# Down products of a fused attention and feed-forward kernel read in two 64-row halves of the array, and key loads with fewer transfers

## The chip, the cores and the metric

The kernel runs on one core of a Trainium2 chip. The metric is the device time of one execution in microseconds (us). Before the change the median of three runs is 2585.47 us, from 2585.27 to 2585.91. The engines are TensorE (PE; its weight loads are shown apart as PEld), VectorE (DVE), ScalarE (ACT), GpSimd (POOL) and SyncE (SP), which here issues the transfers. PSUM has eight banks; a product of up to 512 columns in float32 fills one.

## The reference, cut to what matters

```python
x = A_x                                       # 1 x 2048 x 576
xn = layernorm(x)
q, k, v = split(xn @ wqkv)                    # 32 heads of 18
o = softmax(q @ k.T * 18 ** -0.5) @ v         # per head
s = o @ wo                                    # 576 x 576
f = (gelu(xn @ w_gate) * (xn @ w_up)) @ w_down   # 576 -> 4608 -> 576
out = x + s * silu(f)
```

The product with `w_down` is the "down product" of this document.

## The kernel before

**Precision.** Every factor of a product is held as a high part and a low part in the PE's fast float32 type, and a product is three products: high by high, low by high, high by low. For queries and keys the three stand below one another in one operand of 54 rows (MROW = 3 * 18), and two heads share a tile of 128 rows, one in rows 0 to 63, one in rows 64 to 127.

**Tiles and loops.** Tokens are taken in NB = 4 batches of TB = 512, each of four tiles of 128. F = 4608 is taken in NF = 144 pieces of 128 columns over the four batches: one `section` for each. A prologue (line 162 and others) computes queries, keys and values. Then nine sections (the list FIRST) run ahead of the attention, with the maxima of its first unit among them; then NU * NA = 128 sections (the range ATT) run with the attention spread among them; then the last seven (the epilogue).

**A section** is 27 pairs of gate and up products (line 388), where the gate product reads rows 0 to 63 and the up product rows 64 to 127, each 512 columns wide. Among them stand, in ATT, 16 pairs of one score product (line 729, its exponential on ACT at line 730) and one maximum product (line 698, reduced on DVE at line 699), also one in each half. Behind a section stand, in this order on PE: 16 value products on 32 columns of the array (line 764; a trace shows two instructions for each), at times the small product `max_end` (line 712), at times one output projection of 14 products (`project_o`, line 582), and `downs()`. PE's order is the order of the program; other engines' orders are made by a scheduler.

**The down product.** G = 2 sections make one step r of a batch (NR = 18). Behind a step, `down` is called twice, for token tiles 0 and 1 and for tiles 2 and 3. Each call computes for a tile j and a half c of the 576 outputs (288 columns) a sum of six products over 128 rows, in one PSUM bank `py`, which DVE adds to `Y` (line 432; ACT copies it at line 430 in the first step). In ATT both calls mostly come together (48 products), in other places one call comes behind one section and the other behind the next (24 products).

**Banks.** Tags: "f" has two banks (gate and up products), "m" three (maxima, `acc`, `po`, `max_end`), "s" three (scores, `py`). A tile that is asked for waits until the reader of the tile that had the bank is done.

**Transfers.** SP issues them in order. `load_k` brings a chunk of 512 keys of four heads, `load_q` the queries, one transfer for each of three parts of 18 rows (lines 662 and 687); `load_gu` (line 114) brings the weights of the next section, which POOL splits (lines 94 and 96).

The functions that the change touches:

Of the kernel before, what the change touches and what calls it, by code (L numbers as in the profile page):

```python
# [8 lines left out]
F32 = mybir.dt.float32  # L9
F32R = mybir.dt.float32r  # L10
AF = mybir.ActivationFunctionType
ALU = mybir.AluOpType
# [32 lines left out]
BANKS = {"f": 2, "m": 3, "s": 3}  # L45
# [6 lines left out]
def f(ap):  # L52
    return ap.bitcast(F32)
# [13 lines left out]
def kernel(ctx: ExitStack, tc: tile.TileContext, x, wqkv, wo, w_gate, w_up, w_down, out):  # L67
    nc = tc.nc
    x = x.rearrange("b s d -> (b s) d")
# [18 lines left out]
    identr = const.tile([P, P], F32R, name="identr")  # L88
    nc.gpsimd.tensor_copy(identr, ident)
    all_t = slice(0, TB)  # L90


    def split(hi, lo, raw, keep=lambda i: i):
# [47 lines left out]
    with tc.tile_pool(name="pro", bufs=1) as pro, tc.tile_pool(name="pps", bufs=1, space=PSUM) as pps:  # L141
# [43 lines left out]
        def norm(xr, b, between=None, behind=None):  # L185
            keep = tc.keep_in_program_order if b == 1 else lambda i: i
            st = pro.tile([P, 4, 8], F32, name="st", bufs=2)
            for j in range(4):
                bs = pro.tile([P, 2, 6], F32, name="bs", bufs=2)
                for h in range(2):  # L190
                    one = nc.vector.bn_stats(bs[:, h, :], xr[j][:, 288 * h:288 * h + 288])  # L191
                    keep(one)
                if behind and j == 0:
                    behind(one)
                nc.vector.bn_aggr(st[:, j, 0:2], bs)
            var, r, t = st[:, :, 1], st[:, :, 3], st[:, :, 4]
            nc.scalar.activation(t, var, AF.Sqrt, bias=eps)
            if between:
                between()
            nc.vector.reciprocal(r, t)  # L200
            nc.vector.scalar_tensor_tensor(t, r, -0.5, r, op0=ALU.mult, op1=ALU.mult)
            nc.vector.scalar_tensor_tensor(t, var, EPS, t, op0=ALU.add, op1=ALU.mult)
            nc.vector.scalar_tensor_tensor(r, t, 1.5, r, op0=ALU.add, op1=ALU.mult)
            for j in range(4):
                last = nc.vector.tensor_scalar(xr[j][:, 0:D], xr[j][:, 0:D], st[:, j, 0:1], st[:, j, 3:4],
                                               op0=ALU.subtract, op1=ALU.mult)
                nc.scalar.activation(xr[j][:, D:D + HR], xr[j][:, R0:D], AF.Copy)
            return last
# [42 lines left out]
        def split_qk(t, raw):  # L251
            hi, lo = (pro.tile([P, KT, P], F32R, name=f"q{m}{t}") for m in "hl")
            first = split(hi, lo, raw)
            put_qk(t, hi, lo)
            return first
# [39 lines left out]
                tc.keep_in_program_order(nc.sync.dma_start(wos[i, k * P:k * P + n, :], f(t)[0:n]))  # L295

        NQT = 2 * D // P
        def after(what, before):
            tc.add_manual_dep(what.ins, before.ins.name, mybir.DependencyInfo(
                mybir.DependencyClass.Sync, mybir.DependencyReason.DATA), reason="VectorE alone on the first x")  # L300

        raw_v, ahead_qk, QR = [], [], []
        t = ORDER[0]
        c0 = slice(t * P, (t + 1) * P)
# [17 lines left out]
        last = norm(xr, 0, first_hi, first_loads)  # L322
# [53 lines left out]
    finals = []  # L376

    def gate_up(tag):

        w, xd = FF["w"], FF["xd"]  # L380
        pg, pu = (ps.tile([P, TB], F32, name=n, tag=tag, bufs=BANKS[tag]) for n in ("pg", "pu"))
        terms = [(wp, *divmod(c, XG), xp) for c in range(NC) for wp, xp in ((0, 0), (1, 0), (0, 1))]

        def pair(i):
            wp, k, c, xp = terms[i]
            for a, o in enumerate((pg, pu)):
                rr = slice(HR * a, HR * a + HR)
                nc.tensor.matmul(o, w[1 + wp][k][rr, c, :], xd[xp][k][rr, c, :], start=(i == 0),  # L388
                                 stop=(i == len(terms) - 1))

        return [lambda i=i: pair(i) for i in range(len(terms))], pg, pu
# [6 lines left out]
    def activate(pg, pu, early):  # L398
# [13 lines left out]
            nc.vector.tensor_tensor(t1, t1, pu, op=ALU.mult)  # L412
        return t1

    def down(b, r, hs, wd, Y, js):
        for j in js:
            tt = slice(j * P, (j + 1) * P)
            for c in range(2):
                cc = slice(288 * c, 288 * c + 288)
                tag = "sf"[c if b == NB - 1 and r == NR - 1 else 0]  # L420
                py = ps.tile([P, 288], F32, name="py", tag=tag, bufs=BANKS[tag])
                n = 0
                for g in range(G):
                    hh, hl = hs[g]
                    for a, w in ((hh, wd[0]), (hh, wd[1]), (hl, wd[0])):
                        nc.tensor.matmul(py, a[:, tt], w[:, g, cc], start=(n == 0), stop=(n == 3 * G - 1))  # L426
                        n += 1
                yy = Y[:, j, cc]
                if r == 0:
                    nc.scalar.activation(yy, py, AF.Copy)  # L430
                else:
                    nc.vector.tensor_tensor(yy, py, yy, op=ALU.add)  # L432
                if b == NB - 1 and r == NR - 1:
                    finals.append((Y, j, c))
        if b < NB - 1 and r == NR - 1:
            FF["gates"] += [(b, j, c, Y) for j in js for c in range(2)]

# [70 lines left out]
    op = ctx.enter_context(tc.tile_pool(name="op", bufs=1, reuse_waits="tile"))  # L508
# [98 lines left out]
    for b in range(NB):  # L607
        last = b == NB - 1
# [8 lines left out]
        first = (b + 1) * AB + 3 if last else max((b + 1) * AB + 6, (b + 1) * NR * G - len(FIRST) + 5)  # L617
# [4 lines left out]
        for i in range(GROUPS):  # L622
            n = first + i * (1 if last else G)
# [17 lines left out]
    with tc.tile_pool(name="att", bufs=1, reuse_waits="tile") as att:  # L641
# [8 lines left out]
        def load_k(n, keep=lambda i: i, rs=(0, 1)):  # L650

            u, c = divmod(n, NA)
            if u >= NU:
                return
            cols = slice(c * TB, (c + 1) * TB)
            for r in rs:
                for a in range(2):
                    kk = f(KS[n % KB][r])[64 * a:64 * a + MROW, :]
                    h = QD * (u % NQ) + 2 * r + a
                    rows = slice(D + h * DH, D + (h + 1) * DH)  # L660
                    for n_, i in enumerate((0, 1, 0)):
                        keep(nc.sync.dma_start(kk[n_ * DH:(n_ + 1) * DH, :], qk[i, rows, cols]))

        def load_v(n):

# [11 lines left out]
        def load_q(u, rs=(0, 1)):  # L677
            j, g = divmod(u, NQ)
            cols = slice(j * TB, (j + 1) * TB)
            for r in rs:  # L680
                t = QS[u, r] = att.tile([P, TB], F32R, name=f"q{r}", bufs=3)
                for a in range(2):
                    q = f(t)[HR * a:HR * a + MROW, :]
                    h = QD * g + 2 * r + a
                    rows = slice(h * DH, (h + 1) * DH)
                    for n, i in enumerate((0, 0, 1)):
                        nc.sync.dma_start(q[n * DH:(n + 1) * DH, :], qk[i, rows, cols])
                    nc.sync.dma_start(f(t)[HR * a + MROW:HR * a + HR, :], zq)

        def max_mm(u, i, a):  # L690
# [41 lines left out]
        def lead_pair(s):  # L732

            for a in range(2):
                max_mm(*divmod(s, NS), a)
# [69 lines left out]
        slot, chunk = 0, 1  # L805
        for n, m in enumerate(FIRST):
            none = [lambda: None]
            lead = [lambda s=s: lead_pair(s) for s in range(slot, slot + m)]
            if 0 in NM:
                lead.insert(1, lambda: max_end(0))  # L810
            section((n == 2) * 5 * none + lead + (m > 0 and n != 2) * none, "s" if n == 1 else "f", lead_raw)
            if slot + m >= NS > slot:
                max_neg(0, tc.keep_in_program_order)
            slot += m
            while n > 0 and chunk < KB and chunk * SLOTS <= slot + SLOTS:
                load_k(chunk, tc.keep_in_program_order)
# [34 lines left out]
    with tc.tile_pool(name="epi", bufs=1, reuse_waits="tile") as epi:  # L851
# [4 lines left out]
        n = NU * NA  # L856
# [36 lines left out]
        for Y, j, c in finals:  # L893
            cc = slice(288 * c, 288 * c + 288)
# [7 lines left out]
        for i in range(HIND + 1, GROUPS):  # L902
            th, j, cc = late[i]
# [31 lines left out]
```

## Time and profile before

| | |
|---|---|
| median of three runs | 2585.47 us |
| the profiled execution, its own time | 2584.62 us |
| its span in the profile | 2582.7 us |
| TensorE clock granted | 1.00 |
| VectorE busy | 2010.5 us, 78% |
| ScalarE busy | 1502.5 us, 58% |
| GpSimd busy | 1389.8 us, 54% |

A row of the timeline has the start and the length in us, the engine, the line and the operation, output and inputs, and in brackets how long the engine was idle before it and what ended that. Matmuls are pipelined, so that their lengths overlap: what one costs is the distance from its start to the next start.

### The profile page before, as it was taken

How to read it: one execution, taken by the hardware profiler on the slowest of the kernel's cores; microseconds unless marked ns; L12 is line 12 of the kernel's file. 1: busy time of each engine (PE TensorE's matmuls, PEld its weight loads, DVE VectorE, ACT ScalarE, POOL GpSimd, SP SyncE). 2: the span in 40 equal slices, each digit the busy share in tenths (PEclk: the TensorE clock that was granted, in tenths of full speed). 3: DMA queues.
4: the chain of work that ended last, by engine and by line, in shares of the span. 5: the costliest groups of instructions: out<-in, count | busy, mean ns of one | idle time of the engine just before them, and what ended most of it. 6: DMA issues, size and time to landing. Idle time of an engine off the chain costs nothing.

```text
span 2582.7 us, 56466 instructions
## 1 busy us (share of the span) xinstructions
PE 2575.9 (100%) x20982; PEld 1959.8 (76%) x20982; DVE 2010.5 (78%) x3501; ACT 1502.5 (58%) x2715; POOL 1389.8 (54%) x1506
## 2 busy tenths in 40 slices
PE   9999999999999999999999999999999999999999
PEld 8888777777777777777777777777777777777778
DVE  5326888888887888888888888888888888888445
ACT  3223466666666666565667765556666765566642
POOL 2117554554566465556457565555455755555553
PEclk9999999999999999999999999999999999999999
DMA  8866443344455444544445444445445543545342
GB/s 265 267 237 162 117 104 98 102 105 105 105 135 131 110 114 105 136 111 113 127 114 133 119 125 112 125 112 133 108 109 126 141 114 104 139 110 137 78 117 59
DMA packets 394912, 326.93 MB, mean 127 GB/s; under 512 B 107980, under 2 KB 308684, under 8 KB 394640
## 3 DMA queue, kind: packets, MB, share of 16 engines
q1 hardware_dynamic: 394640, 323.32, 47.3%
q8 instruction: 168, 2.75, 0.5%
q14 instruction: 104, 0.85, 0.1%
HBM read 269.79 MB, written 52.88 MB: 125 GB/s over the span
## 4 chain that ended last, share of the span: by engine, by line
PE 99%; DVE 1%; DMA 0%; POOL 0%; ACT 0%; issue 0%; SPq 0%; DVEq 0%
PE pg L388 25%; PE py L426 18%; PE acc L764 18%; PE pu L388 10%; PE pe L729 9%; PE pm L698 9%; PE po L162 7%; PE po L582 2%; DVE mx L699 0%; PE pt L223 0%; PE pm L712 0%; DMA xx<-in_A_x_dram 0%; DVE bs L191 0%; POOL wh L94 0%; DVE m L706 0%
## 5 line engine op out<-in xcount | busy, mean ns | idle before, releaser
L730 ACT ACTIVATE pT<-pe 128x512 f32<-128x512 f32 x2048 | 1151.6, 599 | 678.4 <-PE pm L698 578.7
L699 DVE TENSOR_REDUCE mx<-pm 128x1 f32<-128x512 f32 x2048 | 1260.0, 683 | 76.4 <-PE pm L698 73.1
L388 PE MATMUL pg<-xd,wh 64*128 64x512 f32 x2592 | 935.5, 393 | 0.0
L388 PE MATMUL pu<-xd,wh 64*128 64x512 f32 x2592 | 935.1, 393 | 0.0
L698 PE MATMUL pm<-KS,q 64*128 64x512 f32 x2048 | 785.2, 388 | 0.2 <-DVE accs L770 0.2
L729 PE MATMUL pe<-q,KS 64*128 64x512 f32 x2048 | 777.9, 387 | 0.0
L94 POOL TENSOR_SCALAR wh<-raw 128x384 fp32r<-128x384 f32 x432 | 228.3, 529 | 610.2 <-PE pu L388 264.0
L388 PEld LDWEIGHTS pg<-xd,wh 64*128 64x128 f32 x2592 | 476.2, 184 | 98.5 <-issue 19.9
L388 PE MATMUL pg<-xd,wl 64*128 64x512 f32 x1296 | 502.0, 387 | 0.9 <-POOL wl L96 0.9
L388 PE MATMUL pu<-xd,wl 64*128 64x512 f32 x1296 | 501.8, 387 | 0.0
L388 PEld LDWEIGHTS pu<-xd,wh 64*128 64x128 f32 x2592 | 477.1, 184 | 22.6
L764 PE MATMUL acc<-pT,VS 128*32 128x512 f32 x4096 | 466.0, 595 | 0.0
L96 POOL TENSOR_TENSOR wl<-raw,wh 128x384 fp32r<-128x384 f32 x432 | 442.1, 1024 | 34.1
L698 PEld LDWEIGHTS pm<-KS,q 64*128 64x128 f32 x2048 | 375.7, 184 | 38.6 <-DVE mx L699 4.9
L729 PEld LDWEIGHTS pe<-q,KS 64*128 64x128 f32 x2048 | 370.1, 184 | 29.9
L432 DVE TENSOR_TENSOR Y<-py,Y 128x288 f32<-128x288 f32 x544 | 248.1, 457 | 161.1 <-PE py L426 160.8
L426 PE MATMUL py<-dh,hh 128*128 128x288 f32 x1152 | 346.0, 300 | 0.0
L426 PE MATMUL py<-dh,hl 128*128 128x288 f32 x1152 | 339.8, 295 | 0.0
L426 PE MATMUL py<-dl,hh 128*128 128x288 f32 x1152 | 339.6, 295 | 0.0
L764 PEld LDWEIGHTS acc<-pT,VS 128*32 128x32 f32 x4096 | 120.5, 109 | 274.5 <-issue 271.2
L388 PEld LDWEIGHTS pg<-xd,wl 64*128 64x128 f32 x1296 | 238.5, 184 | 31.7 <-POOL wl L96 1.2
L388 PEld LDWEIGHTS pu<-xd,wl 64*128 64x128 f32 x1296 | 238.7, 184 | 11.1
(127 smaller groups left out, 2946.5 us busy)
## 6 DMA issues: line engine op xcount, KB each, us to landing
KS<-qk SPq DMA_DIRECT2D x1536, 36.0 KB
raw<-in_B_w_gate_dram SPq DMA_DIRECT2D x144, 288.0 KB
raw<-in_B_w_up_dram SPq DMA_DIRECT2D x144, 288.0 KB
raw<-in_B_w_down_dram SPq DMA_DIRECT2D x68, 576.0 KB
VS<-vs SPq DMA_DIRECT2D x128, 152.0 KB
qk<-t SPq DMA_DIRECT2D x72, 256.0 KB
q<-qk SPq DMA_DIRECT2D x384, 36.0 KB
xd<-xhs SPq DMA_DIRECT2D x24, 384.0 KB
```

The lines of the kernel that those rows point to most:

```text
L94: first = nc.gpsimd.tensor_scalar(hi, raw, 1.0, 1.0, op0=ALU.mult, op1=ALU.mult)
L96: keep(nc.gpsimd.tensor_tensor(lo, raw, f(hi), op=ALU.subtract))
L162: nc.tensor.matmul(o, st, m, start=(i == 0), stop=(i == len(terms) - 1))
L388: nc.tensor.matmul(o, w[1 + wp][k][rr, c, :], xd[xp][k][rr, c, :], start=(i == 0), stop=(i == len(terms) - 1))
L426: nc.tensor.matmul(py, a[:, tt], w[:, g, cc], start=(n == 0), stop=(n == 3 * G - 1))
L432: nc.vector.tensor_tensor(yy, py, yy, op=ALU.add)
L582: nc.tensor.matmul(po[:, 0:288], o[x][:, k, :], ow[w][:, k, :], start=(m == 0), stop=(m == len(terms) - 1))
L698: nc.tensor.matmul(pm, QS[u, r][rr, t * P:(t + 1) * P], KS[(u * NA + c) % KB][r][rr, :], start=True, stop=True)
L699: nc.vector.tensor_reduce(MX[u][:, 2 * r + a, t, c:c + 1], pm, axis=AX.X, op=ALU.max)
L729: nc.tensor.matmul(pe, KS[(u * NA + c) % KB][r][rr, t * P:(t + 1) * P], QS[u, r][rr, :], start=True, stop=True)
L730: nc.scalar.activation(PT[u, kt][:, 2 * r + a, :], pe, AF.Exp, scale=SCALE)
L764: nc.tensor.matmul(ACC[u][32 * a:32 * a + 32, :], VS[(u * NA + c) % VB][:, v:v + 32], pt[:, a, :], start=first, stop=last, skip_group_chec ...
```

## The change

Down products up to the end of ATT (`FF["n"] <= ATT.stop`) are issued as products of 64 rows, two at a time: rows 0 to 63 into the bank of one half c, rows 64 to 127 into the bank of the other, for all six terms of a tile j; then, for both tiles of the call, the same with the halves c changed. A call holds four banks at once, whose tags are given by hand. So that both halves of the array don't write one bank at the same time, an ACT instruction (`mark`) waits for the last pair of a tile's first pass, and the first pair of its second pass waits for `mark`. The adds come behind the second pass. The sums themselves are unchanged. The last eight calls keep the old form.

For keys, the second and third part come in one transfer of 36 rows (the order of the parts changes from high, low, high to high, high, low, and for queries from high, high, low to high, low, high). In FIRST the loads of further key chunks begin one section later. `after` moves to the top of the kernel.

```diff
+    def add_down(b, r, py, Y, j, c):
+        yy = Y[:, j, 288 * c:288 * c + 288]
+        if r == 0:
+            nc.scalar.activation(yy, py, AF.Copy)
+        else:
+            nc.vector.tensor_tensor(yy, py, yy, op=ALU.add)
+        if b == NB - 1 and r == NR - 1:
+            finals.append((Y, j, c))
+
     def down(b, r, hs, wd, Y, js):
-        for j in js:
-            tt = slice(j * P, (j + 1) * P)
-            for c in range(2):
-                cc = slice(288 * c, 288 * c + 288)
-                tag = "sf"[c if b == NB - 1 and r == NR - 1 else 0]
-                py = ps.tile([P, 288], F32, name="py", tag=tag, bufs=BANKS[tag])
-                n = 0
-                for g in range(G):
-                    hh, hl = hs[g]
-                    for a, w in ((hh, wd[0]), (hh, wd[1]), (hl, wd[0])):
-                        nc.tensor.matmul(py, a[:, tt], w[:, g, cc], start=(n == 0), stop=(n == 3 * G - 1))
-                        n += 1
...
+        terms = [(a, w, g) for g in range(G) for a, w in ((0, 0), (0, 1), (1, 0))]
+
+        def product(py, j, c, i, rr=slice(0, P), start=False, stop=False):
+            a, w, g = terms[i]
+            return nc.tensor.matmul(py, hs[g][a][rr, j * P:(j + 1) * P], wd[w][rr, g, 288 * c:288 * c + 288], start=start, stop=stop)
...
+        last = len(terms) - 1
+        if FF["n"] <= ATT.stop:
+            tags = ("sssm", "sssf", "fssm")[0 if FF["n"] <= ATT.start else 1 + js[0] // 2]
+            pys = {(j, c): bank(tags[2 * (j - js[0]) + c]) for j in js for c in range(2)}
+            seen = {}
+            for swap in range(2):
+                for j in js:
+                    for i in range(len(terms)):
+                        for a in range(2):
+                            c = a ^ swap
+                            one = product(pys[j, c], j, c, i, slice(HR * a, HR * a + HR),
+                                          swap == 0 and i == 0, swap == 1 and i == last)
+                            if swap == 1 and i == 0:
+                                after(one, seen[j])
+                    if swap == 0:
+                        seen[j] = nc.scalar.activation(mark, mark, AF.Copy)
+                        after(seen[j], one)
+                    for c in range(2 * swap):
+                        add_down(b, r, pys[j, c], Y, j, c)
+        else:
...
-                    for n_, i in enumerate((0, 1, 0)):
-                        keep(nc.sync.dma_start(kk[n_ * DH:(n_ + 1) * DH, :], qk[i, rows, cols]))
+                    keep(nc.sync.dma_start(kk[0:DH, :], qk[0, rows, cols]))
+                    keep(nc.sync.dma_start(kk[DH:MROW, :], qk[:, rows, cols]))
...
-                    for n, i in enumerate((0, 0, 1)):
-                        nc.sync.dma_start(q[n * DH:(n + 1) * DH, :], qk[i, rows, cols])
+                    nc.sync.dma_start(q[0:2 * DH, :], qk[:, rows, cols])
+                    nc.sync.dma_start(q[2 * DH:MROW, :], qk[0, rows, cols])
...
-            while n > 0 and chunk < KB and chunk * SLOTS <= slot + SLOTS:
+            while n > 1 and chunk < KB and chunk * SLOTS <= slot + SLOTS:
```

More of the change, by code (lines that the diff above doesn't have):

```diff
@@ L90, with after @@
     all_t = slice(0, TB)
+    def after(what, before):
+        tc.add_manual_dep(what.ins, before.ins.name, mybir.DependencyInfo(
+            mybir.DependencyClass.Sync, mybir.DependencyReason.DATA), reason="ordered by hand")
     def split(hi, lo, raw, keep=lambda i: i):
@@ L297 @@
         NQT = 2 * D // P
-        def after(what, before):
-            tc.add_manual_dep(what.ins, before.ins.name, mybir.DependencyInfo(
-                mybir.DependencyClass.Sync, mybir.DependencyReason.DATA), reason="VectorE alone on the first x")
         raw_v, ahead_qk, QR = [], [], []
@@ L376 @@
     finals = []
+    mark = const.tile([P, 1], F32, name="mark")
+    nc.vector.memset(mark, 0.0)
     def gate_up(tag):
@@ L413, in activate @@
         return t1
-    def down(b, r, hs, wd, Y, js):
-        for j in js:
-            tt = slice(j * P, (j + 1) * P)
-            for c in range(2):
-                cc = slice(288 * c, 288 * c + 288)
-                tag = "sf"[c if b == NB - 1 and r == NR - 1 else 0]
-                py = ps.tile([P, 288], F32, name="py", tag=tag, bufs=BANKS[tag])
-                n = 0
-                for g in range(G):
-                    hh, hl = hs[g]
-                    for a, w in ((hh, wd[0]), (hh, wd[1]), (hl, wd[0])):
-                        nc.tensor.matmul(py, a[:, tt], w[:, g, cc], start=(n == 0), stop=(n == 3 * G - 1))
-                        n += 1
[L428 to L434, printed above, removed]
+    def add_down(b, r, py, Y, j, c):
[6 more added lines that the diff above has]
+            finals.append((Y, j, c))
@@ new lines, in down, with bank @@
+    def down(b, r, hs, wd, Y, js):
+        terms = [(a, w, g) for g in range(G) for a, w in ((0, 0), (0, 1), (1, 0))]
+        def product(py, j, c, i, rr=slice(0, P), start=False, stop=False):
+            a, w, g = terms[i]
+            return nc.tensor.matmul(py, hs[g][a][rr, j * P:(j + 1) * P], wd[w][rr, g, 288 * c:288 * c + 288], start=start, stop=stop)
+        def bank(tag):
+            return ps.tile([P, 288], F32, name="py", tag=tag, bufs=BANKS[tag])
+        last = len(terms) - 1
[18 more added lines that the diff above has]
+        else:
+            for j in js:
+                for c in range(2):
+                    py = bank("sf"[c if b == NB - 1 and r == NR - 1 else 0])
+                    for i in range(len(terms)):
+                        product(py, j, c, i, start=(i == 0), stop=(i == last))
+                    add_down(b, r, py, Y, j, c)
```

## Prediction

> **What bounds the kernel now.** I read the page first: the busy line and the chain that ended last.
>
> ```profile
> PE 2575.9 (100%) x20982; PEld 1959.8 (76%) x20982; DVE 2010.5 (78%) x3501; ACT 1502.5 (58%) x2715; POOL 1389.8 (54%) x1506
> ...
> PE 99%; DVE 1%; DMA 0%; POOL 0%; ACT 0%; issue 0%; SPq 0%; DVEq 0%
> PE pg L388 25%; PE py L426 18%; PE acc L764 18%; PE pu L388 10%; PE pe L729 9%; PE pm L698 9%; PE po L162 7%; PE po L582 2%; DVE mx L699 0%; PE pt L223 0%; PE pm L712 0%; DMA xx<-in_A_x_dram 0%; DVE bs L191 0%; POOL wh L94 0%; DVE m L706 0%
> ```
>
> PE alone sets the end, and the down products (py) hold 18% of it. So the time is the sum of the distances between starts on PE, and I read those in PE's timeline of one section with all that stands behind it:
>
> ```profile
> 1201.04 0.39 PE L388 MATMUL pg<-xd,wl 64*128 64x512 f32 x1
> ...
> 1210.13 0.39 PE L388 MATMUL pg<-xd,wh 64*128 64x512 f32 x1
> 1210.44 3.64 PE L764 MATMUL acc<-pT,VS 128*32 128x512 f32 x32
> ...
> 1215.85 0.29 PE L582 MATMUL po<-wol,oh 128*128 128x288 f32 x1
> 1215.98 0.29 PE L426 MATMUL py<-dh,hh 128*128 128x288 f32 x1
> ...
> 1222.21 0.29 PE L426 MATMUL py<-dh,hl 128*128 128x288 f32 x1
> 1222.44 0.49 PE L388 MATMUL pg<-xd,wh 64*128 64x512 f32 x1
> 1222.44 0.49 PE L388 MATMUL pu<-xd,wh 64*128 64x512 f32 x1
> 1222.78 0.39 PE L729 MATMUL pe<-q,KS 64*128 64x512 f32 x1
> ```
>
> From 1201.04 to 1210.13 stand 40 steps between pairs of 64-row products: 9.09 / 40 = 0.2272 us a pair of 512 columns. From 1215.98 to 1222.21 stand 47 steps: 0.1326 us a full product of 288 columns. Where the array goes from full products to 64-row ones it loses time twice: 0.23 to the next start in place of 0.13, and the first pair holds the second off for 0.34 in place of 0.23. I take 0.20 together (the rows are rounded to 0.01). From `po` to `py`, both full, the step is 0.13: nothing is lost.
>
> **The change part by part.** By the code the new form is used in all down calls up to the section n = 136: steps 4 to 66 of 72 in one run of two calls except steps 16, 34 and 52, thus 60 runs of 48 pairs; and 15 single calls of 24 pairs (steps 0 to 3, those three, and one at the end). That is 75 runs, 135 calls and 60 x 48 + 15 x 24 = 3240 pairs in place of 3240 full products. The order of the built program has the same 75 runs at the same places.
>
> *The way back.* Behind each of the 75 runs a section begins, now in the same form of the array: 75 x 0.20 = -15.0 us.
>
> *The way in.* Behind value products the loss stays. In the first seven runs (FIRST) the section itself stands ahead, and both losses go: the last gate pair and the first down product show it, 0.31 in place of 0.23 and then about 0.1 on the second start, as on the way back.
>
> ```profile
> 241.28 0.38 PE L388 MATMUL pu<-xd,wh 64*128 64x512 f32 x1
> 241.59 0.40 PE L426 MATMUL py<-dh,hh 128*128 128x288 f32 x1
> 241.82 0.30 PE L426 MATMUL py<-dl,hh 128*128 128x288 f32 x1
> ```
>
> 7 x 0.20 = -1.4. Against that, 24 runs stand behind a projection (eight in each of three batches), where the step was 0.13: 24 x 0.20 = +4.8; and three stand behind `max_end`: at most 0.2 each, I take +0.5.
>
> *The products.* The trace has no pair of 288 columns. From below: a stretch of the prologue's full products, 126 of 512 columns and 112 of 288,
>
> ```profile
> 44.62 44.32 PE po L162 x238
> ```
>
> gives (44.32 - 112 x 0.1326) / 126 = 0.2339 for a full product of 512 columns, so that a pair of 512 is 0.0067 shorter than one full product; taken off 0.1326 that makes 0.126 for a pair of 288. From above: 0.1326 itself, the row with the same columns, if a pair gains nothing; a limit of another kind is a rival below. I take 0.131, nearer the row with the same width: 3240 x (0.131 - 0.1326) = -5.2 us, with -21 and 0 as ends.
>
> *The marks.* The second pass of a tile begins six pairs behind the end of its first, and its weights load with the start of the pair before: 6 x 0.131 = 0.79 us from the start of the last pair. In that time a product must end (0.29), ACT must see it, `mark` must run, and PE must see that. DVE's add behind a down product, and ACT's smallest operations, give the prices:
>
> ```profile
> 1222.55 0.46 DVE L432 TENSOR_TENSOR Y<-py,Y 128x288 f32<-128x288 f32 x1 [0.34 <-PE py L426]
> 1223.24 1.34 DVE L699 TENSOR_REDUCE mx<-pm 128x1 f32<-128x512 f32 x2 [0.23 <-PE pm L698]
> ```
> ```profile
> L207 ACT ACTIVATE xx<-xx 128x64 f32<-128x64 f32 x16 | 3.8, 252 | 5.2 <-DVE xx L205 5.2
> ...
> L197 ACT ACTIVATE st<-st,eps 128x4 f32<-128x4 f32 x4 | 1.2, 300 | 13.9 <-DVE st L195 13.9
> ```
>
> The add starts 0.34 behind the start of the last product (0.29 and a handover of 0.05); 0.25 to 0.30 for `mark`, 0.05 back: 0.64 to 0.69 of 0.79. ACT must be idle for that, and in ATT it is:
>
> ```profile
> 1212.20 0.63 ACT L407 ACTIVATE t<-t 128x512 f32<-128x512 f32 x1 [0.26 <-DVE t L402]
> 1223.26 1.26 ACT L730 ACTIVATE pT<-pe 128x512 f32<-128x512 f32 x2 [10.44 <-PE pm L698]
> ```
>
> The value products give it 3.6 us to finish the section's work. So 0 in ATT. In the seven runs of FIRST nothing stands between, and in the built program `mark` stands behind the tanh:
>
> ```profile
> 241.54 0.60 ACT L401 ACTIVATE t<-pg 128x512 f32<-128x512 f32 x1 [5.99 <-PE pg L388]
> 242.04 0.59 ACT L405 ACTIVATE t<-pu 128x512 f32<-128x512 f32 x1
> 242.90 0.63 ACT L407 ACTIVATE t<-t 128x512 f32<-128x512 f32 x1 [0.27 <-DVE t L402]
> ```
>
> The tanh ends at 243.53, `mark` some 0.15 later, the pair behind it starts after a handover and its weight load (0.11, below) near 243.8. Unhindered it would start at 241.28 + 0.23 + 12 x 0.131 = 243.1. 7 x 0.7 = +4.9.
>
> *Banks and DVE.* The adds come in two heaps of two a call. Adds that wait follow at 0.37 (an estimate from the two starts below, an add and what follows it without a gap):
>
> ```profile
> 2498.86 0.45 DVE L432 TENSOR_TENSOR Y<-py,Y 128x288 f32<-128x288 f32 x1
> 2499.23 0.68 DVE L412 TENSOR_TENSOR t<-t,pu 128x512 f32<-128x512 f32 x1
> ```
>
> With the last pair at T, tile j = 2 is added from T - 0.45 and T - 0.08, tile 3 from T + 0.34 and T + 0.71, and the first maximum can be reduced at T + 1.08. Before, it was 1223.24 - 1222.21 = T + 1.03, and PE's waits for that are small:
>
> ```profile
> PEld pm L698 <- DVE mx L699: 4.9, 20, 0.4
> ```
>
> The fourth maximum needs the first one's bank, and is due near T + 1.95; the reduction ends at 1.08 + 0.67 = T + 1.75: hidden, with 0.2 left; if that were gone too, each run would lose what is late. The up product needs the "f" bank of (2, 0), free at T + 0.01 and a handover; the second call's first pair needs a bank in the same way. Both are late by 0.01 to 0.03: 60 x 0.03 = +1.8. In the three steps whose calls stand apart, call one's "f" bank is (1, 1), added last: free at T + 1.16 + 0.05, where the next up product wanted its weights at T. 3 x 1.2 = +3.6.
>
> *Transfers.* 640 fewer issues on SP (128 key chunks by four, 64 query tiles by two). PE waits for no transfer, by the chain, so 0, but for one place: the gate and up weights of the fourth section stand behind twelve key issues on SP, so that POOL splits late and PE waits.
>
> ```profile
> 208.66 5.73 SPq L662 DMA_DIRECT2D KS<-qk  x12
> 214.50 0.62 SPq L114 DMA_DIRECT2D raw<-in_B_w_gate_dram  x1
> ```
> ```profile
> PEld pg L388 <- POOL wl L96: 1.2, 1, 1.2
> ```
>
> In the built program those two loads now stand ahead of the keys: -1.1. The keys then issue four fewer and are wanted some 10 us later; not late.
>
> *Sum.* -15.0 - 1.4 + 4.8 + 0.5 - 5.2 + 4.9 + 1.8 + 3.6 - 1.1 = -7.1 us on the profiled execution's own 2584.62: 2577.5. The median of the runs is 0.85 above that execution: 2578.4.
>
> **The rivals.** *No gain from the pair.* It costs 0.1326 like the product: 5.2 us less gain, -1.9 us, 2583.6. For it: the same columns. Against it: pairs of 512 beat full products of 512.
>
> *Slower: `mark` is late in ATT too.* Place: the first pair of each call's second pass, 135 times (the second tile's mark then has the delay as slack). Margin 0.10 to 0.15 us; every 0.1 beyond it costs 13.5 us, and the change turns slower from 0.05 beyond the margin, by more than 0.2% from 0.1. With 0.3 beyond: +33, 2619. For it: no row shows ACT releasing PE with so small an operation. Against it: ACT is idle for 10.44 us there.
>
> *Slower: the pair is held by its instructions.* A pair is two weight loads and two products in 0.131; the most that the trace shows is that in 0.2272. From 0.1332 the change gains nothing, from 0.1348 it is over 0.2% slower; at 0.138, +15.5 us, 2601; at 0.2272, +305. Against it, the weight loads:
>
> ```profile
> 1222.44 0.18 PEld L388 LDWEIGHTS pg<-xd,wh 64*128 64x128 f32 x1 [0.16 <-issue]
> 1222.44 0.18 PEld L388 LDWEIGHTS pu<-xd,wh 64*128 64x128 f32 x1
> 1222.55 0.19 PEld L729 LDWEIGHTS pe<-q,KS 64*128 64x128 f32 x1
> 1222.55 0.19 PEld L698 LDWEIGHTS pm<-KS,q 64*128 64x128 f32 x1
> ```
>
> Both halves load at the same time, and the next pair's loads start 0.11 later: under 0.131. The Trainium skill, "TensorE: Matmul & The Clock Gate", section "Wait — 56ns, not 53.3ns?", has a sequencer cost of about 62 ns for a matmul when hardware decode is off; by it (an estimate) a pair takes at least 124 ns, still under 131, so that this rival would fall; no row here shows a rate past one product in 0.11 us.
>
> **How the numbers follow.** Forecast (pair at 0.126 to 0.132): 0.52, its own range -23 to -3.9 us, 2562.5 to 2581.6. No gain: 0.26. `mark` late: 0.10. Pair held: 0.12. About 0.2%, 5.2 us, is what a measurement of this kernel can tell from no change. Of the forecast's 0.52, 0.04 lies within that bound; of the other cases all of "no gain" falls within it, and of the two slow ones 0.02 (a small excess). Faster 0.48, same 0.32, slower 0.20. The range takes -20 to +13 us: 2565 to 2598; outside are the large ends of the slow rivals and the lowest end of the pair.
>
> **What would show it.** Steps of py64 pairs at 0.131 in PE's timeline; 0.13 and 0.23 at a section's first two starts behind them; no wait of PE for `mark` outside FIRST, and 0.7 seven times within; three waits of 1.2 for the last add; none at the fourth section. Steps of 0.135 or more, or PE waiting for ACT in ATT, would make the prediction wrong.

## The result, and the profile after

The change makes the kernel slower: 2658.86 us (four runs, 2657.31 to 2660.30) against 2585.50 us for the kernel before on the same chip. The ratio is 1.0283, 95% interval 1.0266 to 1.0301. The forecast was 2578.4 us, its range ended at 2598. The profiled execution of the changed kernel took 2660.30 us, 75.7 more than that of before (2584.62).

The page of the changed kernel: busy time, granted clock, and the chain that ended last.

```profile
PE 2605.7 (98%) x24222; PEld 1996.6 (75%) x24222; DVE 1985.3 (75%) x3502; ACT 1541.6 (58%) x2985; POOL 1391.7 (52%) x1506
...
PEclk9998999999999999999999999999999999999999
...
PE 93%; DMA 4%; POOL 2%; DVE 1%; SPq 0%; issue 0%; ACT 0%; POOLq 0%; DVEq 0%; ACTq 0%
PE pg L390 21%; PE py L431 17%; PE acc L793 17%; PE pu L390 12%; PE pe L758 9%; PE pm L727 8%; PE po L166 7%; PE po L611 2%; DMA KS<-qk 2%; DMA raw<-in_B_w_up_dram 1%; DMA q<-qk 1%; DMA xd<-xhs 0%; POOL wl L100 0%; DVE mx L728 0%; PE pt L22
```

The chain was 99% PE. Now 4% of it are transfers, and they are named: keys, up weights, queries. (That is more than PE stands still, since the chain runs through a whole transfer once one sets the end.) So the chain names transfers and not the down products themselves, whose share even fell from 18% to 17%. PE's waits say where the time stands:

```profile
PE py L431 <- POOL hh L98: 22.7, 3, 8.9
PE py L431 <- POOL dl L105: 14.4, 3, 8.8
...
PE py L431 <- ACT mark L453: 2.3, 7, 0.4
...
PEld pu L390 <- DVE Y L422: 15.3, 62, 0.7
```

Columns: total us, times, longest. Before, PE's longest wait in the body was 1.2. Now six long ones, from 2.4 to 8.9, are for POOL's split of the down product's factors (`hh`, `dl`), and some sixty short ones, in PE's weight loads, are for DVE's adds.

**An ordinary run of down products** (PE's and DVE's timeline, the changed kernel):

```profile
1219.87 0.31 PE L431 MATMUL py<-dh,hl 64*128 64x288 f32 x2
...
1224.24 0.32 PE L431 MATMUL py<-dh,hl 64*128 64x288 f32 x2
...
1225.50 1.62 DVE L422 TENSOR_TENSOR Y<-py,Y 128x288 f32<-128x288 f32 x4 [1.70 <-PE py L431]
1225.97 0.29 PE L431 MATMUL py<-dh,hl 64*128 64x288 f32 x2
1226.10 0.40 PE L390 MATMUL pg<-xd,wh 64*128 64x512 f32 x1
1226.37 0.18 PEld L390 LDWEIGHTS pu<-xd,wh 64*128 64x128 f32 x1 [0.21 <-DVE Y L422]
```

Between the first two rows stand 33 steps: 4.37 / 33 = 0.1324 us a pair, what a full product took (0.1326). From the last pair to the section it is 0.13, not 0.23: the way back is as forecast. But the up product's weights, which should load with the gate product's, wait for an add: `pu` starts 0.27 late, and all pairs of the section behind it.

**A stall.** Where a batch ends, its gates (the silu, lines 480 to 482) run on POOL and SP. The first of these places, PE then POOL then SP, the changed kernel:

```profile
819.92 0.29 PE L431 MATMUL py<-dh,hl 64*128 64x288 f32 x2
829.07 0.61 PE L431 MATMUL py<-dh,hh 64*128 64x288 f32 x2 [8.86 <-POOL hh L98]
831.07 0.44 PE L431 MATMUL py<-dl,hh 64*128 64x288 f32 x2
831.31 0.44 PE L431 MATMUL py<-dh,hl 64*128 64x288 f32 x2
```
```profile
820.70 0.51 POOL L98 TENSOR_SCALAR wh<-raw 128x384 fp32r<-128x384 f32 x1 [11.09 <-DMA KS<-qk]
...
823.81 0.83 POOL L480 TENSOR_SCALAR th<-th 128x288 f32<-128x288 f32 x2
...
826.89 1.54 POOL L481 TENSOR_TENSOR th<-th,Y 128x288 f32<-128x288 f32 x2
828.40 0.62 POOL L98 TENSOR_SCALAR hh<-t 128x512 fp32r<-128x512 f32 x1
```
```profile
805.63 1.80 SPq L482 DMA_DIRECT2D ys<-th  x4
...
812.26 0.67 SPq L118 DMA_DIRECT2D raw<-in_B_w_gate_dram  x1
812.98 0.64 SPq L118 DMA_DIRECT2D raw<-in_B_w_up_dram  x1
```

Read backwards: PE waits 8.86 for `hh`; POOL does `hh` last, behind eight operations of the gates and the splits of the next weights; the first of these splits waited 11.09 for its loads, issued at 812.26 and 812.98 behind other transfers. (By the updates of its semaphore the second of them landed at 820.53; the bracket names the keys because their next transfer uses the same semaphore.) Before, POOL did the same operations in the same order, `hh` behind eight of the gates, but in time: the load was issued 17 us ahead of the products and `hh` was done 2.5 us ahead of them (now the load is issued 8 us ahead of 819.92 + 0.13):

```profile
778.54 0.66 SPq L114 DMA_DIRECT2D raw<-in_B_w_gate_dram  x1
...
784.42 0.51 POOL L94 TENSOR_SCALAR wh<-raw 128x384 fp32r<-128x384 f32 x1 [0.76 <-PE pe L729]
...
792.24 0.61 POOL L94 TENSOR_SCALAR hh<-t 128x512 fp32r<-128x512 f32 x1
```
```profile
795.38 0.40 PE L426 MATMUL py<-dh,hh 128*128 128x288 f32 x1
```

Behind the stall the pairs stand 0.24 apart (831.07 to 831.31) in place of 0.1324; more on this in the last section.

**In FIRST** POOL's order itself differs. The changed kernel, then the kernel before:

```profile
220.31 1.42 POOL L98 TENSOR_SCALAR wh<-raw 128x384 fp32r<-128x384 f32 x2 [9.91 <-DMA raw<-in_B_w_up_dram]
...
223.59 1.26 POOL L105 TENSOR_TENSOR hl<-t,hh 128x512 fp32r<-128x512 f32 x1
225.30 2.60 POOL L105 TENSOR_TENSOR dl<-pT,dh 128x1152 fp32r<-128x1152 f32 x1
```
```profile
212.86 1.30 POOL L101 TENSOR_TENSOR hl<-t,hh 128x512 fp32r<-128x512 f32 x1 [2.71 <-ACT hh L100]
214.12 2.66 POOL L101 TENSOR_TENSOR dl<-pT,dh 128x1152 fp32r<-128x1152 f32 x1
220.01 1.18 POOL L94 TENSOR_SCALAR wh<-raw 128x384 fp32r<-128x384 f32 x2 [3.23 <-PE py L426]
```

Before, `dl` came first and the split of the next section's weights (`wh`) behind it. Now the split, which waits 9.91 for its load, stands ahead of the `dl` that PE needs.

**The ledger of the 75.7 us** (each stall as what its stretch took beyond an undisturbed one, slow pairs included): stalls near 218, 253 and 303 us 12.4, 2.9 and 6.0; near 820, 1464 and 2102 12.3, 9.7 and 10.6; near 1412 and 214 3.5 and 0.9: 58. Banks: a section behind a down run takes 9.93 against 9.56 unhindered, 0.37 x 60 = 22. Marks 5, steps from full products into pairs 5; the way back and the way in -14, the wait at the fourth section -1. Together 75.

### The profile page after: what moved, and what is told of

It reads as the page before. It is cut to its first block, busy times and chain, and to the rows that moved or that the text cites. A ratio compares the mean times of both kernels' runs of the same rounds, so it can differ in the third digit from the quotient of the medians.

```text
span 2658.5 us, 62467 instructions
## 1 busy us (share of the span) xinstructions
PE 2605.7 (98%) x24222; PEld 1996.6 (75%) x24222; DVE 1985.3 (75%) x3502; ACT 1541.6 (58%) x2985; POOL 1391.7 (52%) x1506
## 4 chain that ended last, share of the span: by engine, by line
PE 93%; DMA 4%; POOL 2%; DVE 1%; SPq 0%; issue 0%; ACT 0%; POOLq 0%; DVEq 0%; ACTq 0%
PE pg L390 21%; PE py L431 17%; PE acc L793 17%; PE pu L390 12%; PE pe L758 9%; PE pm L727 8%; PE po L166 7%; PE po L611 2%; DMA KS<-qk 2%; DMA raw<-in_B_w_up_dram 1%; DMA q<-qk 1%; DMA xd<-xhs 0%; POOL wl L100 0%; DVE mx L728 0%; PE pt L227 0%
## 5 line engine op out<-in xcount | busy, mean ns | idle before, releaser
L759 ACT ACTIVATE pT<-pe 128x512 f32<-128x512 f32 x2048 | 1139.9, 598 | 284.0 <-PE pe L758 189.5
L758 PE MATMUL pe<-q,KS 64*128 64x512 f32 x2048 | 769.5, 390 | 0.0
L727 PE MATMUL pm<-KS,q 64*128 64x512 f32 x2048 | 759.5, 388 | 0.9 <-DMA pT<-in_B_w_down_dram 0.7
L431 PE MATMUL py<-dh,hh 64*128 64x288 f32 (+1 forms) x2232 | 371.5, 304 | 25.6 <-POOL hh L98 22.7
L422 DVE TENSOR_TENSOR Y<-py,Y 128x288 f32<-128x288 f32 x544 | 222.2, 452 | 223.9 <-PE py L431 223.5
L431 PE MATMUL py<-dl,hh 64*128 64x288 f32 (+1 forms) x2232 | 362.0, 296 | 14.4 <-POOL dl L105 14.4
L431 PE MATMUL py<-dh,hl 64*128 64x288 f32 (+1 forms) x2232 | 362.1, 296 | 1.5 <-POOL hl L100 1.5
L453 ACT ACTIVATE mark<-mark 128x1 f32<-128x1 f32 x270 | 54.7, 203 | 444.9 <-PE py L431 444.4
L431 PEld LDWEIGHTS py<-dh,hh 64*128 64x128 f32 (+1 forms) x2232 | 239.6, 189 | 69.9 <-issue 37.4
```

The source lines that it names most:

```text
L431: return nc.tensor.matmul(py, hs[g][a][rr, j * P:(j + 1) * P], wd[w][rr, g, 288 * c:288 * c + 288], start=start, stop=stop)
L453: seen[j] = nc.scalar.activation(mark, mark, AF.Copy)
L727: nc.tensor.matmul(pm, QS[u, r][rr, t * P:(t + 1) * P], KS[(u * NA + c) % KB][r][rr, :], start=True, stop=True)
L758: nc.tensor.matmul(pe, KS[(u * NA + c) % KB][r][rr, t * P:(t + 1) * P], QS[u, r][rr, :], start=True, stop=True)
L759: nc.scalar.activation(PT[u, kt][:, 2 * r + a, :], pe, AF.Exp, scale=SCALE)
```

## The experiments

All times are medians, ratios are against the kernel before on the same chip. The runs ask in turn which part of the change costs time, by which mechanism, and whether the repairs add up.

### Each part alone

**e1: the new down form alone**, keys, queries and their order as before (three transfers, `n > 0`).

> The kernel before with only the new down product; keys and queries still come in three transfers and the key loads of FIRST begin where they did. In the changed kernel's trace about 58 us lie in a few places where PE waits for POOL's splits (12.7 at 218, 2.9 at 253, 6.0 at 303, 12.3 at 820, 9.7 at 1464, 10.6 at 2102, 3.2 at 1415, with the slow steps behind them). Theory T (the new transfers reorder SP and POOL): these go, 2658.9 - 58 = about 2601. Rival D (the new down form reorders them): they stay, about 2655 to 2660. Both: the pu waits of 0.25 us for the last add stay, 60 times.

Measured 2611.20, ratio 1.0099 (1.0084 to 1.0115): +25.7, 10 above the first forecast. The long stalls are gone: PE's longest wait for a split is 1.0.

**e2: the transfers alone**, down products as before.

```diff
-                    for n_, i in enumerate((0, 1, 0)):
-                        keep(nc.sync.dma_start(kk[n_ * DH:(n_ + 1) * DH, :], qk[i, rows, cols]))
+                    keep(nc.sync.dma_start(kk[0:DH, :], qk[0, rows, cols]))
+                    keep(nc.sync.dma_start(kk[DH:MROW, :], qk[:, rows, cols]))
```

(queries and `n > 1` likewise)

> The kernel before with only the new transfers of keys and queries and the later start of the key loads in FIRST; down products as before. Theory T: the stalls of some 58 us are here, 2635 to 2645. Rival D: no stall over 2 us, 2583 to 2587, as I reckoned the transfers at nothing.

Measured 2612.16, ratio 1.0099 (1.0082 to 1.0116): +26.6. Fewer transfers, the part that was put down at nothing, cost as much as the down form. The time lies between the two forecasts: the stalls are there, but not all of the 58 us. PE's waits in this kernel are of the kind of the stalls above:

```profile
PE py L426 <- POOL dl L101: 11.3, 3, 8.1
PE py L426 <- POOL hh L94: 4.5, 2, 2.7
```

The two parts alone make 52.3, together 73.4: the other 21 come from their meeting. Most of it shows at the gates, where PE's waits for `hh` grow from 1.0 (e1) and 4.5 (e2) to 22.7; why they grow so was not tried apart.

### The banks

**e3: the changed kernel, e4: e1, with the banks of ATT dealt otherwise**: of the two calls of a step the first takes "ssff", the second "smss", so that both "f" banks are free early.

```diff
-            tags = ("sssm", "sssf", "fssm")[0 if FF["n"] <= ATT.start else 1 + js[0] // 2]
+            more = bool(FF["down"]) and FF["down"][0][-1] < FF["n"]
+            tags = "smss" if FF.pop("half", False) else "ssff" if more and FF["n"] > ATT.start else "sssm"
+            FF["half"] = tags == "ssff"
```

> The changed kernel with other banks in ATT alone: a call pair takes s s f f and then s m s s, so that the next section's gate and up products take banks that were added over 3 us earlier; calls that stand apart take s s s m. SP and POOL keep the changed kernel's order. If the 0.25 us at each up product is the wait for its bank: 62 waits (15.3 us) and three of 0.5 go, 2641 to 2643. Rival: DVE's late adds hold the next maxima instead and the wait only moves, 2655 to 2659.

> The first kernel of this call (down form alone) with the banks of the third. Theory T and the banks together: 2601 - 17 = about 2584, that is within 3 us of the kernel before. Rival D: about 2640.

e3 2648.05, 1.0241 (1.0226 to 1.0256); e4 2598.65, 1.0049 (1.0034 to 1.0064): 10.8 and 12.6 gained, about half of the 22 and less than forecast. PE's weight loads in e4 show the other half:

```profile
PEld pe L760 <- DVE Y L422: 11.5, 55, 0.2
```

The up product no longer waits, the score product does, for an "s" bank. By the order of the built program DVE adds the half c = 1 of a tile ahead of c = 0, so the bank of (2, 0) comes free one add later than the hand-dealt tags assume.

**e6: e1 with the banks dealt by the order of the adds**: the second call takes "msss" in place of "smss".

> The down form alone with banks s s f f and m s s s in place of s m s s. In the built program DVE adds the column half c = 1 of a tile ahead of c = 0, so that the sum (2, 0) comes second and is free at T + 0.35 (T: start of the last pair), where I had reckoned T + 0.01; in the run before it held the first score product by 0.2 us, 60 times. Now the bank of (2, 1) is wanted first: 2598.7 - 10 = 2588.5 if so, 2597 to 2600 if the first product is held by something else.

Measured 2590.78 (ten runs, 2585.15 to 2592.68; the trace is of the fastest), ratio 1.0018 (1.0009 to 1.0028): 7.9 less than e4, 20.4 less than e1. The wait is gone, and the section behind a run takes 9.56. That settles the banks: their waits cost 20, where the forecast had 1.8 and 3.6. Freeing both "f" banks early gave 12.6 of it, following the order of the adds 7.9.

### The order on POOL, and the marks in FIRST

**e5: the changed kernel with one POOL split held behind `dl`** in the sections n = 2, 4, 6, 8 of FIRST; SP's order is the same.

```diff
-                split_gu(nxt, k)
+                split_gu(nxt, k, tc.keep_in_program_order if k == 0 and n in (2, 4, 6, 8) else lambda i: i)
```

> The changed kernel, with SP's order and all transfers as they are, but in FIRST four splits (the first of the sections n = 2, 4, 6, 8) pinned on POOL behind what stands ahead of them in the code, so that the low halves of the down weights (dl) are split before the next gate and up weights, which wait for their loads. If POOL's order makes the stalls of FIRST, those at 218, 253 and 303 go (12.7 + 2.9 + 6.0 us in the changed kernel's trace): about 2637. Rival: the transfers themselves are late and PE waits elsewhere for the same loads: 2652 to 2660. The stalls at 820, 1464 and 2102 stay by both.

Measured 2654.45, ratio 1.0264 (1.0247 to 1.0281): 4.4 gained where the three stalls of FIRST cost 21, as the rival had it. In its trace PE's wait at 218 shrinks from 8.8 to 2.3 and those at 253 and 303 go, but PE then waits 4.2 at 288, and shorter times behind it and at 251, for the splits of the gate and up weights. POOL's order turns a late load into a stall; with the order mended the load is still late. So POOL's order alone is not the cause.

**e7: e6 with the old down form in FIRST, and the gates' POOL and SP work written behind the section's end**:

```diff
-        if FF["n"] <= ATT.stop:
+        if ATT.start < FF["n"] <= ATT.stop:
...
-            nc.gpsimd.tensor_scalar(th, th, 1.0, 1.0, op0=ALU.add, op1=ALU.mult)
-            nc.gpsimd.tensor_tensor(th, th, Y[:, j, cc], op=ALU.mult)
-            nc.sync.dma_start(ys[rows, cc], th)
+            FF["late"].append((th, Y[:, j, cc], ys[rows, cc]))
...
+            late_gates()
```

> The run before with two more edits: old down form in FIRST (no mark there, 7 x 0.9 us, against 7 x 0.2 for the switch), and POOL's part of the gates traced behind the section's splits, so that hh no longer stands behind eight gate operations (waits of 2.8 + 1.1 + 1.1 us with slow steps behind them, about 7). 2588.5 - 5 - 7 = 2576 to 2578, faster than the kernel before by 0.3%. Rival: with POOL's order mended PE waits for the late loads themselves, 2583 to 2589.

Measured 2581.47 (ten runs), ratio 0.9985 (0.9975 to 0.9994): 9.3 less than e6, between the two forecasts, and below the kernel before. The two edits were not tried apart.

### What makes the loads late

**e8: the changed kernel, e9: e2, with the 36-row transfers written row by row**: the same bytes in the same number of transfers, the 18 rows outside and the two parts inside.

```diff
-                    keep(nc.sync.dma_start(kk[DH:MROW, :], qk[:, rows, cols]))
+                    keep(nc.sync.dma_start(kk[DH:MROW, :], qk[:, rows, cols].rearrange("i p t -> p i t")))
...
-                    nc.sync.dma_start(q[0:2 * DH, :], qk[:, rows, cols])
-                    nc.sync.dma_start(q[2 * DH:MROW, :], qk[0, rows, cols])
+                    nc.sync.dma_start(q[0:DH, :], qk[1, rows, cols])
+                    nc.sync.dma_start(q[DH:MROW, :], qk[0, rows, cols].rearrange("p (o t) -> p o t", o=1).to_broadcast([DH, 2, TB]))
```

> The changed kernel with the same number of key and query transfers at the same places, but the 36-row ones written row by row: hi and lo of a row lie next to each other (the queries then hold lo, and hi twice), so that a transfer's outer count is 18 and not 2. In the changed kernel's trace a 36-row key transfer gives 3 updates of its semaphore and lands 5.4 us after its issue, an 18-row one of the kernel before gives 10 and lands in 2.1; the gate weights behind them land in 4.9 in place of 3.5. Theory L (the 36-row transfer is worked off by few DMA engines, all that lies behind it lands late, and PE's stalls come from that): it gives 10 updates or more, lands in 2 to 3.5 us, and the time falls to that of the down form alone, 2600 to 2615. Rival O (SP's and POOL's order alone makes the stalls; it is kept here): 2650 to 2660.

> The kernel before with the new transfers alone, the 36-row ones written row by row as in the run above. Theory L: the 26.6 us of the transfers alone go, 2583 to 2590. Rival O: 2606 to 2616, as with the transfers alone.

e8 2635.49, 1.0192 (1.0178 to 1.0206), 23.4 gained; e9 2595.01, 1.0039 (1.0024 to 1.0055), 17.2 gained. Both lie between the two forecasts. SP's and POOL's orders did not move, so what was gained is the form of the transfer: 23.4 of 73.4, and 17.2 of 26.6. The rest has other causes. The traces give the time from the end of an issue to the last update of the transfer's semaphore (median us, 300 to 2400):

```
                 before  after   e8     e2     e9
keys, 18 rows     2.07    4.67   2.42   4.40   2.04
keys, 36 rows      -      5.39   1.94   5.14   1.86
gate weights      3.48    4.92   4.67   4.38   3.54
values (VS)       2.25    5.22   2.04   5.39   2.11
maxima (q<-mr)    1.05    2.44   1.05   2.22   1.05
```

A transfer of 36 rows in the changed kernel sends 3 updates, one of 18 rows, or of 36 rows written row by row, 10. So fewer ends have to come in, and yet it lands 2.6 times as late as the 18-row one did before (5.39 against 2.07); what is issued around it becomes late too, the values by 3.0, the maxima by 1.4. The Trainium skill, "DMA: Bandwidth & Descriptors", section "Why a DMA increments its semaphore by 16 and not by 1", says that the number of engines has to divide the outermost dimension of the access pattern: a dimension of size 2 leaves a transfer two engines. The trace agrees by its counts, 3 against 10, if one update comes at once and one from each engine: two engines against nine. In e8 the gate weights stay late (4.67), and the stalls at the gates stay too; in e9, without the new down form, they land in 3.54. Why the two differ was not tried. What SP lost by the slow transfers shows in its waits, changed kernel and then e8 (25.0 before):

```profile
SPq L814 <- DMA oT<-accs: 68.1, 31, 5.0
```
```profile
SPq L814 <- DMA oT<-accs: 20.7, 27, 2.1
```

Which of the late transfers costs how much of the 23 us was not tried.

e9's remaining 9.7 are one stall, in FIRST, for a `dl` that stands behind the split:

```profile
PE py L426 <- POOL dl L101: 7.3, 1, 7.3
```

### Do the repairs add up

**e13: e8 with the gates' work written late** as in e7.

> The changed kernel with the 36-row transfers row by row (2635.5 us) and one edit more: POOL's part of the gates traced behind the section's splits, so that hh stands ahead of the gate operations. Its three stalls at 810, 1446 and 2083 cost 7.6 + 8.5 + 6.9 us there. If POOL's place for hh makes them: 2635.5 - 15 to 23 = 2613 to 2620. Rival: the loads of the gate and up weights are late on SP, hh waits behind their splits just the same: 2628 to 2636.

Measured 2621.34, ratio 1.0140 (1.0125 to 1.0155): 14.2 gained, with a few moves in SP's order beside the edit. The three stalls at the gates fall from 7.6, 8.5 and 6.9 to 1.6, 6.4 and 0.5.

**e10: the changed kernel with all of it**: row-by-row transfers, late gates, banks by the order of the adds, old form in FIRST.

> The changed kernel with the banks in the order of the adds, the old down form in FIRST, POOL's gates behind the section's splits, and the 36-row transfers row by row. Theory L: as the mended kernel with three transfers or better, 2572 to 2582. Rival O: the reordered loads cost 10 to 30 us over it, 2590 to 2612.

Measured 2598.06, ratio 1.0048 (1.0035 to 1.0060). That is the rival's forecast. Most of the 13 that are left above the kernel before stand in one place again, PE's wait at 218:

```profile
PE py L431 <- POOL dl L105: 8.2, 1, 8.2
```

**e11: e10 with the POOL split held in section n = 2 alone. e14: in n = 2, 4, 6, 8.**

> The run before (all mended, 36-row transfers row by row) with one split pinned on POOL: the first of section n = 2 behind the low halves of the first down weights (dl). In the built program nothing else moves on POOL and nothing on SP. If POOL's order alone makes the stall at 218 (8.6 us, and 2.9 us of pairs at half the clock behind it), it goes: 2598.1 - 11.5 = 2586.5. Rival: PE waits at the next section for the gate and up weights whose splits are now later by 4 us: 2590 to 2595.

> All mends together with the change's two transfers: 36-row transfers row by row, banks by the order of the adds, old down form in FIRST, gates behind the splits, and the first split of the sections n = 2, 4, 6, 8 pinned on POOL. With one pin the stall only moved from 218 to 241 (8.1 us). If POOL's order in FIRST is all that is left, 2595.4 - 8 = 2587, and less than 3 us over the kernel before. Rival: the loads behind it are late and the stall moves on again: 2592 to 2597.

e11 2595.42, 1.0039 (1.0024 to 1.0054): the stall shrank and moved, it did not go. At 218 the products now start within a microsecond; 24 us later, one section on:

```profile
240.96 0.40 PE L431 MATMUL py<-dh,hh 128*128 128x288 f32 x1
...
245.97 0.61 PE L431 MATMUL py<-dl,hh 128*128 128x288 f32 x1 [4.62 <-POOL dl L105]
```

With all four held, e14 takes 2588.56 (ten runs), 1.0017 (1.0007 to 1.0027). This is the forecast of POOL's order, not of its rival. So the 73.4 come apart along one chain of repairs: form of the transfers 23.4, gates' order 14.2, banks and old form in FIRST 23.3, POOL's splits in FIRST 9.5; 3.1 are left.

**e12: e7 with the one part of the transfers that was forecast to gain**, the key loads that begin a section later.

```diff
-            while n > 0 and chunk < KB and chunk * SLOTS <= slot + SLOTS:
+            while n > 1 and chunk < KB and chunk * SLOTS <= slot + SLOTS:
```

> The mended kernel with three transfers (2581.5), with the key loads of FIRST begun one section later as in the change. In the built program only one pair of gate and up loads moves ahead of twelve key issues on SP. PE's wait of 1.43 us at the fourth section's first low product should go: 2580. Rival: the keys are then late for the first maxima: 2581.5 or more.

Measured 2580.56 (eleven runs, 2579.19 to 2582.08) against 2584.78, ratio 0.9982 (0.9973 to 0.9991): faster than the kernel before by 4.2 us, and the best of all. From e7 it can't be told apart. Its page and a way back from pairs to a section:

```profile
PE 2570.1 (100%) x24054; PEld 1945.7 (75%) x24054; DVE 1980.0 (77%) x3502; ACT 1550.8 (60%) x2971; POOL 1391.1 (54%) x1506
...
PE 97%; DVE 2%; DMA 0%; issue 0%; ACT 0%; POOL 0%; SPq 0%; DVEq 0%; ACTq 0%
```
```profile
1218.03 0.31 PE L431 MATMUL py<-dh,hl 64*128 64x288 f32 x2
1218.16 0.39 PE L390 MATMUL pg<-xd,wh 64*128 64x512 f32 x1
1218.17 0.39 PE L390 MATMUL pu<-xd,wh 64*128 64x512 f32 x1
1218.39 0.39 PE L765 MATMUL pe<-q,KS 64*128 64x512 f32 x1
```

`pg` and `pu` start together, 0.13 behind the last pair, and the third start follows 0.23 later: nothing is lost on the way back.

## Why the prediction was wrong, and where it was right

- **"PE waits for no transfer, by the chain, so 0"** failed, and it is the largest term. The chain of before shows that PE waits for none *as they were issued and shaped then*. The step counted issues (640 fewer) and left out how a transfer of another shape lands. Even the count was no relief: an issue of 36 rows took 0.61 us in place of 0.31, so that a head's keys cost SP 0.99 in place of 0.94. The transfers alone cost 26.6; written row by row 9.7 (e2, e9).
- **What is behind the late load** was not asked. Raw weights are loaded into a buffer that POOL's split frees, so that a late load delays the split, the split the next load, and on POOL everything behind it. The prediction compared the order of the two built programs on PE, and named SP's order for the fourth section alone; the new order on POOL in FIRST (splits ahead of `dl`) stood in the built program and was worth 9.5 (e10 to e14). At the gates POOL's order was the old one, `hh` behind the gates; it cost nothing while the loads came in time, and moving `hh` ahead then gained 14.2 (e8 to e13).
- **"The up product needs the 'f' bank of (2, 0), free at T + 0.01"**: the place was right, the size wrong. The adds did begin where forecast (T - 0.47, with T = 1225.97), but (2, 1) is added first, and (2, 0) is free at T + 0.35. The two bank terms, this one of 1.8 and the next of 3.6, measured 20 together (e1 to e6).
- **"Call one's 'f' bank is (1, 1), added last ... 3 x 1.2"**: the same order of adds made these waits 0.71 behind call one and 0.36 behind call two, 3 x 1.07 in place of 3 x 1.2: the sum was near, the place half right.
- **The pair at 0.131**: it is 0.1324. The rival "no gain from the pair" was right on this, the term -5.2 falls away. By the prediction's estimate a pair of 512 columns gains on a full product, and one of 288 does not; why, no run here settles. The rival "held by its instructions" is out.
- **The way back, 75 x 0.20**: right. In e12, where no bank hinders it, the gap falls from 0.224 to 0.126 and the section behind the run from 9.666 to 9.562: 0.20. In the changed kernel the bank wait eats the second half and 0.26 more: the section takes 9.93.
- **Full products into pairs, + 4.8 and + 0.5**: right. Behind a projection the first step goes from 0.131 to 0.220 and the second from 0.133 to 0.238, 0.19 together, 4.7 for 24; behind `max_end` 0.15 each.
- **Marks**, and the way in ahead of them: in FIRST a run that no stall hides takes 0.48 more than before, the gain of the way back left aside, as forecast (0.7 - 0.2; the pair behind `mark` starts at 243.91, forecast 243.8); the rival "late in ATT too" fell, but for three gate steps, where ACT's tanh stands ahead of `mark` and 0.5 each are lost.
- **"None at the fourth section", -1.1**: the wait for `wl` is gone in the changed kernel and stays in e1 (0.7). Right.
- **The sum**: with the transfers and orders mended (e12) the design yields -4.2, not -7.1. The way back's -13 (66 runs) and the fourth section's -1 are given back by 5 where full products stand ahead, 1.5 for marks, and 4.3 in 27 sections behind `max_end`, which went on average from 9.70 to 9.86 (27 x 0.16) and had no term; the rest, under 1, has no name. The changed kernel still takes 9.70 there, e6 9.75 and e7 9.83, so that this cost came with the repairs. What grows there is the wait of the maximum products for the "m" bank that DVE's `accs` frees, kernel before and then e12:

```profile
PEld pm L698 <- DVE accs L770: 1.5, 4, 0.6
```
```profile
PEld pm L734 <- DVE accs L806: 6.7, 19, 0.6
```

## What to carry to other kernels

A term of zero needs its cover written beside it: "PE waits for no transfer" holds for the shapes and the issue order of that trace, so when a transfer's shape changes, cost its landing, and when a scheduler rebuilds the program, compare the order on every engine and queue that feeds the critical one, and the slack of what stands there. Banks dealt by hand should follow the order in which the built program frees them, not the order of the source. And a wait in a loop that refills its own buffer is not cured where it shows: holding one POOL operation moved the stall by a section (e11).

## What the runs showed of the hardware

**A transfer's form counts more than the number of transfers.** The same 36 rows landed in 5.39 us with the two parts outside and in 1.94 with the rows outside, and the slow form held up transfers of other buffers as well.

**A stall costs more than its wait.** Behind the stall at 820 the granted clock is 0.5. Two windows of the changed kernel (columns: window, us, busy time of PE, PEld, DVE, ACT, POOL with counts, granted clock; the last two, on transfers, are not used here):

```profile
815.00:819.00 4.00, 4.00 (x38) 1.48 (x38) 3.61 (x6) 3.04 (x6) 0.00 (x0) 1.00 1.25 174
...
829.00:833.00 4.00, 3.43 (x26) 3.09 (x28) 0.00 (x0) 0.41 (x2) 3.75 (x6) 0.50 0.32 85
```

Five stretches of half clock stand in its trace, of 6.83, 10.24 (three times) and 13.65 us, all multiples of 3.41. None follows the wait of 2.4 at 253, one follows the wait of 3.1 at 303. PE runs 5 to 6 us at 0.24 a pair after it resumes, some 2.4 us lost each time. The Trainium skill, "TensorE: Matmul & The Clock Gate", section "Part 1: The HAM clock gate", has the clock halved after an idle window of about 3.4 us, with windows that run free. The multiples agree, and the five stretches begin 25, 152, 188 and 187 windows of 3.413 apart. That a whole window has to be idle the trace does not bear out: in the 3.41 us ahead of the half clock at 305.73 PE stood still for 1.73 only, and in e11 for 1.59 ahead of one at 802.27. How much is enough these runs do not say: a window with 1.72 idle, at 254.52 on the same grid, brought none.

**Short pairs gain nothing from being split.** A pair of 64-row products of 288 columns takes what one full product takes (0.1324 against 0.1326); the only gain is where a change of form goes away, 0.10 on the first start and 0.10 on the second, and a new change costs as much.
